# Three 64-partition loads issued by ScalarE, and the last quarter of the second weights issued by GpSimd inside tile 0's second product

## The chip, the core and the metric

The kernel runs on one core of a Trainium2 chip. The core's engines are TensorE (PE, matmuls; its weight loads are listed as PEld), VectorE (DVE), ScalarE (ACT), GpSimd (POOL) and SyncE (SP). They run their own instruction streams in order and wait for each other by semaphores. Transfers between HBM and the on-chip memory are started by an instruction on SP, ACT or POOL and are carried out by 16 DMA engines that all of them share. The profile names the queues by their issuer: q1 is SP's, q10 is ACT's (both "hardware_dynamic"), q0 is POOL's ("software_dynamic").

The metric is device time in microseconds (us), lower is better. Beside the plain runs there is one profiled execution, from which all rows below come.

## What is computed

Attention in a sliding window, then a feed-forward block with the tanh form of GELU:

```python
# q, k, v: 8 batches x 8 heads x 576 positions x 64, fp32
scores = q @ k^T / 8;  scores = -1e9 where |i - j| > 32
attn = softmax(scores);  a = attn @ v
x = a.transpose(0, 2, 1, 3).reshape(4608, 512)
h = x @ w_in                      # w_in 512 x 2048
out = gelu_tanh(h) @ w_out        # w_out 2048 x 512
```

## The kernel before

The 4608 tokens are worked on in nine tiles of 512. While the second product (`gelu @ w_out`) of tile t runs on TensorE, the attention of batch t+1 is woven into it at fixed places. All engines' orders are written out by hand: what the Python code emits first on an engine runs first on it.

Inputs arrive in fp32 and are cast to fp16 on chip. `w_in` and `w_out` are loaded in four quarters of 1 MB each (`load_w_in`, `load_w_out`, lines 232 to 238) into fp32 staging buffers `wst` (a ring of five, shared with the values `vr`) and cast by `cast_w` (line 240, profile line L242) on DVE, ACT or POOL. Below, wo0 to wo3 are the four quarters of `w_out`; each holds four blocks of 128 rows, so wo2 holds blocks 8 to 11 and wo3 blocks 12 to 15. A quarter can be loaded in two halves of 512 KB; wo2b is the second half of wo2 (line 856), wo3a and wo3b are the halves of wo3 (lines 858 and 860).

All loads of the opening are issued by SP, except two of the very first (one of q, one of k), which ACT issues. Loads to 64 partitions carry the last 64 positions of a batch, 128 KB each in rows of 256 bytes: `vs(4)` loads those of v (`vt`, line 156), `tails_0("q")` those of q of batch 0 (`tr`, line 166), `tails_0("k")` those of k. In SP's order the stretch that matters reads:

```python
850    wo.append(load_w_out(1, stage_w()))          # wo1, 1 MB
851    qk(4)
852    tails_0("q")                                 # 64 partitions
853    wo.append(load_w_out(2, stage_w(), 0, 2))    # wo2a
854    qk(6)
855    vs(0)
856    load_w_out(2, wo[2], 2, 4)                   # wo2b
857    vs(1)
858    wo.append(load_w_out(3, stage_w(), 0, 2))    # wo3a
859    vs(2, 3)
860    load_w_out(3, wo[3], 2, 4)                   # wo3b
861    vs(4)                                        # 64 partitions
862    tails()
```

Here `qk(4)` is one 256 KB load of q and one of k for two heads of batch 1, and `vs(0)` to `vs(3)` are the four 256 KB loads of batch 1's values. After line 862 SP goes on to batch 2 (`load_qk(2)`).

Loads by SP and ACT share eight completion semaphores in turn, in the order in which they are recorded: each load waits, before it is issued, for the landing of the load eight places before it. So wo2b waits for wo1, and wo1 is what SP waits for before it can issue wo2b.

Tile 0's second product is 64 steps (`ffn_out_0`, profile line L691), one matmul each. `ORDER_0` (line 70) gives the order: four steps for each block of `w_out`, so step i below 48 needs block i // 4, roughly; blocks 12 to 15 are needed from step 48 on (12 and 13 from 48, 14 and 15 from 56). `PLAN_0` (line 53) says before which step each other action comes. Those that matter here: `w1` at 15 (casts of wo1), `k2` at 19 (casts of q and k of batch 1, and POOL's cast of batch 0's q tail, L334), `w2` at 28 (blocks 8 and 9 of wo2), `t-1` at 29 and `s-1` at 34 (batch 0's tail), `n0` at 34 (sums of batch 1, their logarithm and reciprocal on ACT), `e0`, `e1`, `e2`, `e3` at 35, 43, 47, 52 (POOL's casts of the values, L329), `k3` at 37, `w5` at 38 (blocks 10 on POOL and 11 on ACT), `r3` at 41, `s3` and `w3` at 47 (blocks 12 on DVE and 13 on POOL), `d0` to `d3` (DVE copies of the values), `u3` at 55 (blocks 14 on POOL and 15 on ACT), `p0` at 57 (batch 1's weighted values), `e4` at 58 (POOL's cast of `vt`).

Of the kernel before, what the change touches and what calls it, by code (L numbers as in the profile page):

```python
# [78 lines left out]
def kernel(  # L79
# [9 lines left out]
    nc = tc.nc  # L89
    B, H, S, D = q.shape  # L90
# [12 lines left out]
    def load_table(which):  # L103
        nc.scalar.add_instruction(mybir.InstLoadActFuncSet(  # L104
            name=nc.get_next_instruction_name(), act_func_set_id=which, ins=[], outs=[]))
# [29 lines left out]
    raws, vrs = {}, {}  # L135

    def load_early(b):


        qr = rawp.tile([128, H, 256], FP32, name="qr")  # L140
        kr = rawp.tile([128, H, 256], FP32, name="kr")
        raws[b] = [qr, kr, None]

        def qk(h0, queues=(nc.sync, nc.sync)):
            for src, dst, queue in zip((q, k), (qr, kr), queues):
                queue.dma_start(
                    dst[:, h0:h0 + 2, :],
                    src[b, h0:h0 + 2, 0:512, :].rearrange("h (p j) d -> p h (j d)", j=4))

        def vs(*cs):  # L150
            if len(raws[b]) < 4:
                raws[b].append(stage.tile([128, 4, H, 64], FP32, name="vr", tag="stage"))
                raws[b].append(tailp.tile([64, H, 64], FP32, name="vt", tag="vt"))
            for c in cs:
                if c == 4:
                    nc.sync.dma_start(raws[b][4], v[b, :, 512:S, :].rearrange("h p d -> p h d"))
                else:
                    nc.sync.dma_start(raws[b][3][:, c, :, :],
                                      v[b, :, 128 * c:128 * c + 128, :].rearrange("h p d -> p h d"))

        def tails(which="qk"):
            if raws[b][2] is None:
                raws[b][2] = tailp.tile([128, H, 64], FP32, name="tr", tag="tr")
            tr = raws[b][2]
            if "q" in which:
                nc.sync.dma_start(tr[0:64, :, :], q[b, :, 512:576, :].rearrange("h s d -> s h d"))
            if "k" in which:
                nc.sync.dma_start(tr[64:128, :, :], k[b, :, 512:576, :].rearrange("h s d -> s h d"))

        return qk, tails, vs  # L170

    def load_qk(b):
# [54 lines left out]
    w_out_v = moe_w_out.rearrange("(c p) f -> p c f", p=128)  # L227

    def stage_w():
        return stage.tile([128, 4, 512], FP32, name="wst", tag="stage")  # L230
# [2 lines left out]
        nc.sync.dma_start(w[:, c0:c1, :], w_in_v[:, c0:c1, 512 * i:512 * i + 512])  # L233
        return w

    def load_w_out(i, w, c0=0, c1=4):
        nc.sync.dma_start(w[:, c0:c1, :], w_out_v[:, 4 * i + c0:4 * i + c1, :])
        return w

    def cast_w(w, dst, on_dve=(0, 1), cs=range(4), on_act=()):  # L240
        for c in cs:
            (nc.scalar.copy if c in on_act else nc.vector.tensor_copy if c in on_dve else nc.gpsimd.tensor_copy)(  # L242
                dst[:, c, :], w[:, c, :])

    qk, tails_0, vs = load_early(0)
# [3 lines left out]
    qk(4)  # L249
    qk(6)  # L250
    load_table(exp_set)
    def v_of_pair(g, hs=(0, 1)):
        for h in (2 * g + x for x in hs):
            nc.sync.dma_start(raws[0][3][:, :, h, :], v[0, h, 0:512, :].rearrange("(c p) d -> p c d", p=128))  # L254

    vs(4)
    for g in range(3):
        v_of_pair(g)
    wi = [stage_w()]
    load_w_in(0, wi[0], 0, 2)  # L260
    for x in range(2):
        v_of_pair(3, (x,))
        load_w_in(0, wi[0], 2 + x, 3 + x)
# [43 lines left out]
    def band_out():  # L307
        blocks(nc.vector.tensor_copy, band, full, even, (0, 1, 24, 8), (24, 3, 32, 0), (120, 1, 24, 0))
        blocks(nc.vector.tensor_copy, band, full, odd, (0, 1, 40, -8), (40, 2, 32, 0), (104, 1, 40, 0))
# [9 lines left out]
    def cast_early(b, pr, engs):  # L319
        for src, dst, eng in zip(raws[b][0:2], halfs[b][0:2], engs):  # L320
            if eng is not None:
                eng.tensor_copy(dst[:, pr, :, :, :].rearrange("p j h d -> p h j d"),
                                src[:, 2 * pr:2 * pr + 2, :].rearrange("p h (j d) -> p h j d", j=4))
# [78 lines left out]
    def open_and_turn(b):  # L402
        cast_open(b)
        turn_queries(b, raws[b][0], halfs[b][0], 0, 128)
# [74 lines left out]
    def weigh(b, g, pair=None):  # L479
        pe = groups.pop((b, g))  # L480
        if pair is not None:
            od = psS.tile([128, 2, 512], FP32, name="ps_od", tag=f"S{pair}")
            o, d = od[:, 0, :], od[:, 1, :]
        else:
            o = psO.tile([128, 512], FP32, name="ps_o", tag="O")
            d = psO.tile([128, 512], FP32, name="ps_d", tag="D")
        sum_up(b, g, d, pe)
        times(b, g, o, pe)
        return o, d
# [36 lines left out]
    def ffn_in(t, n, d0=0, d1=4, then=True):  # L526
        fc = column(t, n)
        if t not in gTs:
            gTs[t] = gp.tile([128, NF, 512], FP16, name="gT", tag="gT")
        if d0 == 0:  # L530
            if t == 0:
                i = n % 8
                if i in (4, 6):
                    phs["S"] = psS.tile([128, 2, 512], FP32, name="ph2", tag=f"S{i // 2 - 2}")
                phs[fc] = psO.tile([128, 512], FP32, name="ph", tag="DO"[i]) if i < 2 else \
                    bank(i - 2) if i < 4 else phs["S"][:, i % 2, :]
            else:
                i = 3 if n in (1, 2) else 0 if n == 0 else (2, 1, 0)[n % 3] if t < NT - 2 else (2, 0)[n % 2 if n > 3 else 0]
                if n == 1:
                    phs["S"] = psS.tile([128, 2, 512], FP32, name="ph3", tag="S0")  # L540
                phs[fc] = bank(i) if i < 2 else phs["S"][:, n - 1, :] if i == 3 else \
                    psO.tile([128, 512], FP32, name="ph", tag="D")
        ph = phs[fc]
        for dc in range(d0, d1):
            nc.tensor.matmul(ph, w_in16[:, dc, fc * 128:fc * 128 + 128],  # L545
                             xT[:, dc, t * 512 % RING:t * 512 % RING + 512],
                             start=(dc == 0), stop=(dc == 3))
        if d1 == 4 and then:
            gelu(t, n)

    def gelu(t, n):
        fc = column(t, n)
        nc.scalar.activation(gTs[t][:, fc, :], phs[fc], AF.Gelu_apprx_tanh)  # L553
        if t and n % 4 == 3:
            sums(t, n // 4)
# [263 lines left out]
    values(0, nc.gpsimd.tensor_copy)  # L819
    values(1, nc.gpsimd.tensor_copy)  # L820

    qk, tails, vs = load_early(1)
    qk(0)
    wo = [load_w_out(0, stage_w())]
    qk(2)

# [21 lines left out]
    cast_w(wi[1], w_in16[:, :, 512:1024], (0, 2))  # L848
    cast_w(wi[2], w_in16[:, :, 1024:1536], (0, 2))
    wo.append(load_w_out(1, stage_w()))  # L850
    qk(4)
    tails_0("q")
    wo.append(load_w_out(2, stage_w(), 0, 2))
    qk(6)
    vs(0)
    load_w_out(2, wo[2], 2, 4)
    vs(1)
    wo.append(load_w_out(3, stage_w(), 0, 2))
    vs(2, 3)
    load_w_out(3, wo[3], 2, 4)  # L860
    vs(4)
    tails()

    cast_open(1)
# [2 lines left out]
    def quarter(i, *dcs):  # L867
        for dc in dcs:
            for n in range(4 * i, 4 * i + 4):
                ffn_in(0, n, dc, dc + 1, then=False)  # L870
        if 3 in dcs:
            for n in range(4 * i, 4 * i + 4):
                gelu(0, n)

    quarter(1, 0, 1, 2, 3)
    cast_w(wi[3], w_in16[:, :, 1536:2048], (0, 2))
    quarter(2, 0, 1, 2, 3)
    cast_early(1, 0, split)
    band_out()
    quarter(3, 0, 1)  # L880
# [13 lines left out]
    for t in range(NT):  # L894
        b = t + 1
# [55 lines left out]
        for i in range(113 if t else 65):  # L951
# [3 lines left out]
            if t == 1 and i == 94:  # L955
                for c in range(4):
                    nc.gpsimd.tensor_copy(Vs[1][:, c, :, :], vrs[3][:, c, :, :])
            if t == 1 and i == 98:
                open_and_turn(3)
            for act in plan.get(i, "").split():  # L960
                kind, at = act[0], int(act[act.index("@") + 1:]) if "@" in act else None
                g = int(act[1:].split("@")[0])
                if kind == "w":
                    if g == 3:
                        cast_w(wo[g], w_out16[:, 12:16, :], cs=(0, 1), on_dve=(0,))
                    else:
                        cast_w(wo[g % 3], w_out16[:, 4 * (g % 3):4 * (g % 3) + 4, :], on_act=(1, 3),
                               cs={1: range(4), 2: (0, 1), 5: (2, 3)}[g])
# [41 lines left out]
                elif kind == "v":  # L1010
                    bb, gg = group(g)
                    o, d = weigh(bb, gg, at)
# [61 lines left out]
```

## Time and profile before

| what | value |
|---|---|
| runs | 299.73, 299.79, 300.87 us; median 299.79 us |
| profiled execution, device time | 298.71 us |
| its span, first to last instruction | 297.0 us |
| its granted TensorE clock | 0.999 |
| PE busy | 287.1 us (97%) |
| DVE, ACT, POOL busy | 209.2 us (70%), 196.4 us (66%), 89.4 us (30%) |
| share of the 16 DMA engines' span: q1, q0, q10 | 61.6%, 23.0%, 1.1% |
| moved | 51.01 MB, 172 GB/s on average |

Stretches of the opening, from the view by windows (busy us of each engine in the stretch, then the DMA engines' busy share and rate):

| stretch, us | PE | DVE | ACT | POOL | DMA share | GB/s |
|---|---|---|---|---|---|---|
| 0 to 4 | 2.74 | 1.55 | 2.10 | 1.78 | 0.44 | 144 |
| 8 to 12 | 3.65 | 2.87 | 3.45 | 1.82 | 1.28 | 248 |
| 20 to 24 | 4.00 | 1.54 | 2.61 | 1.65 | 1.06 | 400 |
| 32 to 34 | 1.41 | 0.86 | 1.29 | 0.49 | 1.07 | 372 |
| 38 to 40 | 1.96 | 1.64 | 1.46 | 0.46 | 1.09 | 245 |
| 42 to 44 | 2.00 | 1.31 | 1.41 | 0.00 | 1.13 | 307 |
| 46 to 48 | 1.52 | 0.22 | 1.66 | 1.22 | 1.18 | 276 |
| 48 to 50 | 2.00 | 1.82 | 0.57 | 0.97 | 0.67 | 153 |
| 52 to 54 | 1.49 | 1.81 | 2.00 | 0.75 | 1.11 | 219 |

The page reads so: engine busy times are sums over instructions; the DMA share is the time that packets took as a share of the 16 engines' time, and can exceed 1 because packets overlap. In the timeline a row is: start, duration, engine, line, operation, output and input, count, and in brackets the idle time of that engine before the row and what ended it. SPq, ACTq and POOLq rows are the issues of loads and stores, not the transfers. Some SPq durations hold waiting as well as issuing.

### The profile page before, as it was taken

The page shows a single profiled execution, that of the slowest core. Times are in us where ns is not written, and L with a number is a line of the kernel's source. Part 1 is how long each engine was busy: PE and PEld are TensorE (multiplying, and loading weights), DVE is VectorE, ACT ScalarE, POOL GpSimd, SP SyncE. Part 2 cuts the span into 40 slices and gives each one's busy share as a digit, 9 for nine tenths or more (in the row PEclk, how much of TensorE's full clock was granted, in tenths as well). Part 3 has the DMA queues.
Part 4 walks back from the last instruction along what each step waited for, and adds up shares of the span by engine and source line. Part 5 has one row for each costly group of instructions (what it writes and reads, how often), then busy time and mean ns, then how long its engine had stood idle before and what let it go on. Part 6 is the DMA issues. An engine that isn't in the chain of part 4 may idle for free.

```text
span 297.0 us, 7282 instructions
## 1 busy us (share of the span) xinstructions
PE 287.1 (97%) x2949; PEld 184.7 (62%) x2949; DVE 209.2 (70%) x466; ACT 196.4 (66%) x315; POOL 89.4 (30%) x141
## 2 busy tenths in 40 slices
PE   7889999999999999999999999999999999999993
PEld 3534444446874587458844884488547867786783
DVE  4662475997986676868686879576966776964772
ACT  4876756778587876678657965695669557705800
POOL 3435415201407731406080606060800050015000
PEclk9999999999999999999999999999999999999999
DMA  7999999989999998989997997999594040004013
GB/s 216 263 297 383 366 280 263 264 178 202 291 192 191 235 233 156 145 167 244 150 193 116 253 145 158 142 227 170 102 175 38 0 116 29 2 13 131 0 35 109
DMA packets 116615, 51.01 MB, mean 172 GB/s; under 512 B 98391, under 2 KB 110167, under 8 KB 116582
## 3 DMA queue, kind: packets, MB, share of 16 engines
q1 hardware_dynamic: 91684, 38.67, 61.6%
q0 software_dynamic: 23776, 10.83, 23.0%
q10 hardware_dynamic: 1122, 1.06, 1.1%
q8 instruction: 23, 0.38, 0.6%
q14 instruction: 10, 0.08, 0.1%
HBM read 36.70 MB, written 9.44 MB: 155 GB/s over the span
## 4 chain that ended last, share of the span: by engine, by line
PE 80%; DMA 13%; DVE 2%; SPq 2%; ACT 1%; issue 1%; POOL 0%
PE mm L719 32%; PE mm L545 17%; PE ph L545 15%; DMA wst<-in_moe_w_out_dram 7%; DMA wst<-in_moe_w_in_dram 5%; PE pu L597 3%; PE ps_s L436 3%; PE ps_d L463 2%; DMA tr<-in_k_dram 2%; PE ps_o L473 2%; SPq L254 2%; PE mm L597 1%; PE ps_od L473 1%; PE ps_od L463 1%; PE mm L691 1%; PE py L719 1%
## 5 line engine op out<-in xcount | busy, mean ns | idle before, releaser
L545 PEld LDWEIGHTS <-w_in 128*128 128x128 f16 x512 | 49.7, 98 | 56.9 <-POOL w_in L835 0.5
L545 PE MATMUL ph<-xT,w_in 128*128 128x512 f16 x256 | 64.1, 379 | 0.4 <-POOL w_in L835 0.4
L545 PE MATMUL mm<-xT,w_in 128*128 128x512 f16 x256 | 64.1, 379 | 0.0
L681 POOL DMA_DIRECT2D out_dram<-y x55 | 32.3, 597 | 83.8 <-DVE y L748 75.5
L553 ACT ACTIVATE gT<-mm 128x512 f16<-128x512 f32 x60 | 35.6, 598 | 33.1 <-PE mm L545 32.5
L719 PEld LDWEIGHTS <-s 128*128 128x128 f16 x512 | 49.3, 98 | 7.1 <-DVE s L662 0.6
L719 PE MATMUL mm<-t,s 128*128 128x256 f16 x376 | 45.2, 273 | 0.3 <-DVE y L732 0.2
L662 DVE TENSOR_TENSOR s<-gT 128x512 f16<-128x512 f16 x64 | 27.2, 426 | 19.0 <-ACT gT L553 18.8
L719 PEld LDWEIGHTS <-gT 128*128 128x128 f16 x384 | 36.2, 98 | 6.5
L553 ACT ACTIVATE gT<-ph 128x512 f16<-128x512 f32 x58 | 32.2, 600 | 10.9 <-PE ph L545 10.9
L449 ACT ACTIVATE pe<-ps_s 128x960 f16<-128x960 f32 (+1 forms) x31 | 29.5, 974 | 13.9 <-PE ps_s L436 13.8
L719 PE MATMUL mm<-w_out,gT 128*128 128x256 f16 x256 | 32.6, 273 | 0.0
L104 ACT ACT_TABLE_LOAD x18 | 23.1, 1283 | 2.2 <-issue 1.9
L498 ACT ACTIVATE lt<-ps_d 128x480 f32<-128x480 f32 (+2 forms) x28 | 15.6, 556 | 10.4 <-PE ps_d L463 6.9
L499 ACT ACTIVATE lt<-lt 128x480 f32<-128x480 f32 (+3 forms) x36 | 21.1, 585 | 1.1
L458 DVE TENSOR_TENSOR pe<-pe,band 128x960 f16<-128x960 f16 x28 | 18.6, 683 | 2.3 <-ACT pe L449 2.3
L473 PEld LDWEIGHTS <-V 128*64 128x64 f16 x520 | 13.8, 111 | 6.3 <-DVE V L218 1.2
L719 PE MATMUL mm<-t,gT 128*128 128x256 f16 x128 | 16.1, 273 | 0.0
L208 POOL DMA_DIRECT2D V<-in_v_dram x16 | 14.3, 909 | 1.1 <-POOL after L953 0.4
L662 DVE TENSOR_TENSOR s<-s,gT 128x512 f16<-128x512 f16 x32 | 13.9, 434 | 1.1
L719 PE MATMUL mm<-w_out,s 128*128 128x256 f16 x120 | 14.6, 273 | 0.0
L508 DVE TENSOR_TENSOR xT<-ps_o,lt 128x480 f16<-128x480 f32 (+5 forms) x26 | 13.4, 536 | 1.1 <-PE ps_o L473 1.1
(146 smaller groups left out, 387.1 us busy)
## 6 DMA issues: line engine op xcount, KB each, us to landing
kr<-in_k_dram SPq DMA_DIRECT2D x31, 256.0 KB, 10.0
qr<-in_q_dram SPq DMA_DIRECT2D x6, 1024.0 KB, 6.9
wst<-in_moe_w_in_dram SPq DMA_DIRECT2D x7, 512.0 KB, 8.4
wst<-in_moe_w_out_dram SPq DMA_DIRECT2D x2, 1024.0 KB, 11.6
wst<-in_moe_w_out_dram SPq DMA_DIRECT2D x4, 512.0 KB, 5.8
qr<-in_v_dram SPq DMA_DIRECT2D x8, 256.0 KB, 5.6
V<-in_v_dram POOLq DMA_DIRECT2D x16, 128.0 KB, 8.8
qr<-in_q_dram SPq DMA_DIRECT2D x7, 256.0 KB, 6.9
```

The costliest lines, as they stand in the source:

```text
L104: nc.scalar.add_instruction(mybir.InstLoadActFuncSet(name=nc.get_next_instruction_name(), act_func_set_id=which, ins=[], outs=[]))
L208: nc.gpsimd.dma_start(V[:, c, :, :], v[b, :, 128 * c:128 * c + 128, :].rearrange("h p d -> p h d"))
L449: nc.scalar.activation(pe, ps[:, :, 0:w], AF.Exp, scale=SCALE)
L458: nc.vector.tensor_tensor(pe, pe, m.rearrange("k (o j) p -> k o j p", o=1).broadcast_to(list(pe.shape)), op=ALU.mult)
L473: nc.tensor.matmul(o[64 * h:64 * h + 64, cols].rearrange("d (j p) -> d j p", j=4)[:, :, p0 - q0:p1 - q0], Vs[b % 2][:, slot, 2 * pr + h, : ...
L498: nc.scalar.activation(lt[:, 0:n], d[:, 0:n], AF.Ln)
L499: nc.scalar.activation(lt[:, 0:n], lt[:, 0:n], AF.Exp, scale=-1.0)
L545: nc.tensor.matmul(ph, w_in16[:, dc, fc * 128:fc * 128 + 128], xT[:, dc, t * 512 % RING:t * 512 % RING + 512], start=(dc == 0), stop=(dc = ...
L553: nc.scalar.activation(gTs[t][:, fc, :], phs[fc], AF.Gelu_apprx_tanh)
L662: nc.vector.tensor_tensor(dst, x, y, op=op)
L681: eng.dma_start(out_v[b, j, q0 + p:q0 + p + e, cols], yo[m:m + e, cols])
L719: nc.tensor.matmul(pys["apart"][:, 0:256] if apart else py[:, blk, :], lhsT, wino[w][:, f, :], start=(new and i % (8 if one else 16) == 0) ...
```

## The change

Three loads to 64 partitions go from SP to ACT. The one of batch 0's v tail is recorded after the first table load instead of just before it in SP's order; that of batch 0's q tail stands in ACT's order after the twelve GELUs of the first three quarters of tile 0's first product; that of batch 1's v tail stands before step 30 of tile 0's second product. The two halves of wo3 go from SP to POOL, before step 20 of the same product, so after POOL's cast of the q tail (`k2`, step 19). Every other load keeps its place in SP's order. `vs` and `tails` and `load_w_out` get the issuing queue as an argument.

```diff
-        def vs(*cs):
+        def vs(*cs, queue=nc.sync):
...
                 if c == 4:
-                    nc.sync.dma_start(raws[b][4], v[b, :, 512:S, :].rearrange("h p d -> p h d"))
+                    queue.dma_start(raws[b][4], v[b, :, 512:S, :].rearrange("h p d -> p h d"))
...
-        def tails(which="qk"):
+        def tails(which="qk", queue=nc.sync):
...
             if "q" in which:
-                nc.sync.dma_start(tr[0:64, :, :], q[b, :, 512:576, :].rearrange("h s d -> s h d"))
+                queue.dma_start(tr[0:64, :, :], q[b, :, 512:576, :].rearrange("h s d -> s h d"))
...
-    def load_w_out(i, w, c0=0, c1=4):
-        nc.sync.dma_start(w[:, c0:c1, :], w_out_v[:, 4 * i + c0:4 * i + c1, :])
+    def load_w_out(i, w, c0=0, c1=4, queue=nc.sync):
+        queue.dma_start(w[:, c0:c1, :], w_out_v[:, 4 * i + c0:4 * i + c1, :])
...
     load_table(exp_set)
+    vs(4, queue=nc.scalar)
...
-    vs(4)
     for g in range(3):
         v_of_pair(g)
...
-    qk, tails, vs = load_early(1)
+    qk, tails, vs_1 = load_early(1)
...
     qk(4)
-    tails_0("q")
     wo.append(load_w_out(2, stage_w(), 0, 2))
     qk(6)
-    vs(0)
+    vs_1(0)
     load_w_out(2, wo[2], 2, 4)
-    vs(1)
-    wo.append(load_w_out(3, stage_w(), 0, 2))
-    vs(2, 3)
-    load_w_out(3, wo[3], 2, 4)
-    vs(4)
+    vs_1(1)
+    wo.append(stage_w())
+    vs_1(2, 3)
     tails()
...
     quarter(2, 0, 1, 2, 3)
+    tails_0("q", nc.scalar)
     cast_early(1, 0, split)
...
+            if t == 0 and i == 20:
+                load_w_out(3, wo[3], 0, 2, nc.gpsimd)
+                load_w_out(3, wo[3], 2, 4, nc.gpsimd)
+            if t == 0 and i == 30:
+                vs_1(4, queue=nc.scalar)
```

## The prediction

> **What bounds the kernel now.** I read the chain that ended last first. By engine (page, part 4):
>
> ```profile
> PE 80%; DMA 13%; DVE 2%; SPq 2%; ACT 1%; issue 1%; POOL 0%
> ```
>
> TensorE carries it but for 13% of transfers. In order of time, these lie in the opening alone:
>
> ```profile
> 17.35 9.12 DMA wst<-in_moe_w_in_dram
> 26.55 11.24 DMA wst<-in_moe_w_out_dram
> 37.81 8.40 DMA wst<-in_moe_w_out_dram
> 46.26 0.62 POOL w_out L242
> 46.92 0.38 PE mm L691
> ```
>
> (Start, length, what.) wo1 lands at 37.8, which lets SP issue wo2b; wo2b lands 8.4 us later, POOL casts block 10 in 0.62 us, and step 40 starts at 46.92. From there the chain is TensorE's. The timeline of TensorE shows what its waits in tile 0's second product are worth:
>
> ```profile
> 33.96 0.60 PE L691 MATMUL mm<-w_out,gT 128*128 128x512 f16 x2 [0.59 <-DVE w_out L242]
> ...
> 46.92 0.38 PE L691 MATMUL mm<-w_out,gT 128*128 128x512 f16 x1 [0.48 <-POOL w_out L242]
> ...
> 52.85 0.38 PE L691 MATMUL mm<-w_out,gT 128*128 128x512 f16 x1 [0.40 <-POOL w_out L242]
> ```
>
> The three (wo0, block 10 of wo2, block 14 of wo3) sum to 1.47 us: all that better loading here can give back. SP's own timeline:
>
> ```profile
> 37.81 2.18 SPq L237 DMA_DIRECT2D wst<-in_moe_w_out_dram  x1
> 40.04 1.06 SPq L158 DMA_DIRECT2D vr<-in_v_dram  x1
> 41.20 2.28 SPq L237 DMA_DIRECT2D wst<-in_moe_w_out_dram  x1
> 43.53 2.64 SPq L158 DMA_DIRECT2D vr<-in_v_dram  x2
> 46.21 2.42 SPq L237 DMA_DIRECT2D wst<-in_moe_w_out_dram  x1
> ```
>
> The reader is to see the order: wo2b (37.81) stands in front of both halves of wo3 (41.20, 46.21), and q1 serves them in that order. Last, what q1 moved from 42 to 46.2, while wo2b was on its way (packets, MB, share of 16 engines):
>
> ```profile
> q1 hardware_dynamic: 1944, 1.26, 105.3%
> ```
>
> The DMA engines are full, at 0.30 MB a us. So transfers and their order bound step 40, not issuing.
>
> **Part by part: wo3 from POOL.** POOL's timeline says when it can issue:
>
> ```profile
> 37.85 0.61 POOL L242 CAST w_out<-wst 128x512 f16<-128x512 f32 x1 [1.97 <-DMA wst<-in_moe_w_out_dram]
> 40.94 0.60 POOL L334 CAST t<-tr 64x512 f16<-64x512 f32 x1 [2.47 <-DMA tr<-in_q_dram]
> ```
>
> The cast at 37.85 waits for wo1. L334 follows it, and waits no more: its tail now travels from about 31, and ACT's first loads were cast 3.8 to 4.6 us after issue (0.81 to 4.58, 1.35 to 5.92). So L334 ends at 39.1. Then the two issues: nearest rows 0.65 us (128 rows of 2 KB, L681) and 0.91 us (1024 rows of 256 B, L208); these have 256 rows of 2 KB, I take 0.65, so 1.3 (at most 1.8) us. POOL idles 3.04 us ahead of its next cast (44.58), which hides them; without that idle they would delay `e0`, not TensorE. The buffer of wo3 came free at 30.2 (last casts of `w_in`), so the issues wait for nothing.
>
> From issue to transfer, POOL's stores show 1 to 3 us (117.40, with 0.38 MB moved from 118 to 120; 76.42, with only 0.08 MB before 80). The transfer thus starts between 40.3 and 42; I take 42. wo2b then still has 1.26 MB of q1 ahead of and in itself. How do q0 and q1 share? The nearest row is POOL's store beside SP's k loads. From 78 to 80, nearly alone:
>
> ```profile
> q1 hardware_dynamic: 1688, 0.50, 109.5%
> ```
>
> and from 80 to 82, together:
>
> ```profile
> q1 hardware_dynamic: 951, 0.24, 54.3%
> q0 software_dynamic: 133, 0.43, 53.4%
> ```
>
> q0 took half of the engines' time and q1's bytes halved. At these rates wo3 (1.05 MB at 0.215 MB a us) needs 4.9 us, to 46.9. In that time q1 moves half of 0.30 x 4.9, some 0.74 MB; the other 0.52 MB takes 1.7 us more. wo2b lands at 48.6 instead of 46.2: +2.4 us. Upper bound: all of wo3 first, 1.05 MB at the 0.37 MB a us of 32 to 34, +2.8. Lower bound: q0 starts after 46.2, 0; below nothing, -0.5, if the tail's 128 KB, which stood before wo2b, moved in otherwise unused engine time. I take 2.4, as the start can slip to 44 and still leave +2.2. TensorE already waits at step 40, so all of this counts: it starts at 46.92 + 2.4 = 49.3.
>
> The Trainium skill's page "DMA: Bandwidth & Descriptors", section "Issuing engines are not separate DMA queues", says that loads of all issuers run on the same 16 engines and interleave, and that more issuers save issue time only; that speaks against this change, and the windows above agree (q1 from 0.50 to 0.24 MB). By that rule with equal turns the sum would be near the upper bound, by the rows it is the 2.4.
>
> What it saves: wo3 lands at 46.9, before steps 48 and 56 want it, so the 0.40 at 52.85 goes.
>
> **What comes behind.** With wo3 gone, batch 1's values follow wo2b in q1: 256 KB each, 0.85 us apiece at 0.30 MB a us, 49.5, 50.3 and 51.2. POOL's last value cast (0.61 to 1.09 us) is then over by 52.3 and DVE's last two copies (0.29 to 0.60 each) by 53.5; `p0`, at 53.16 before, comes at 55.2. This has 1.7 us of cover. q of batch 2 is issued earlier than 50.70; its cast at 58.75 waited for no transfer.
>
> **SP's freed places.** The five issues took 0.61 (4.95), 1.57 (30.12), 2.28, 2.42 and 0.61 (48.67) us. Those after wo2b free nothing that TensorE waits for; the first two lie before it, but wo2b's issue waits for wo1's landing (SP idles 0.77 us before 37.81), and bytes before wo1 stay the same, less nothing and plus the q tail, which now runs beside wo1 instead of behind it: 128 KB, 0.35 us at 0.37 MB a us. That delays block 4 (cast 37.94 to 38.74, step 16 at 38.86) by up to 0.35 us, and is swallowed by the wait at step 40, as is any delay ahead of it.
>
> **The three issues on ACT.** Each 0.50 us (ACTq rows at 0.81 and 1.35: 0.50, 0.49). The v tail of batch 0 goes at 3.16, before six copies; ACT idles 1.11 us before its next row (5.89). It now runs beside the last q and k loads instead of behind them: 512 packets at 760 a us (q1, 10 to 12 us: 1520 packets in 2 us), 0.67 us against the same gain for the values behind; bounds -0.6 to +0.7, and I take 0. The q tail goes at 30.8 into idle times of 0.87 and 0.71 us (before 31.68 and 32.98); its semaphore is that of q's first load of batch 1, cast at 30.15. So 0, and still 0 at SP's 1.57 us for the same load. The v tail of batch 1 adds a wait: it shares its semaphore with `qk(6)`'s k load, eight places earlier. Before, that landed by 44.5 (its cast at 44.51 idled for nothing); at half rate from 42 I put it at 45.5. ACT stands still from 44.1 to 46.0. Queued behind: exp of the tail (0.60), two Ln (1.03), two Exp (1.09), block 11's cast (0.62), so until 49.4; step 44 stood 1.31 us behind step 40 (48.23 and 46.92), so it wants block 11 at 49.3 + 1.3 = 50.6. Hidden, with 1.2 us to spare.
>
> **Sum.** +2.4 - 0.40 + 0 = +2.0 us. The profiled execution (span 297.0, 1.7 around it, 298.71) becomes 300.7. The median of the runs lies 1.08 above it; I carry the difference over: 299.79 + 2.0 = 301.8 us. About 0.5%, 1.5 us, is what a measurement of this kernel can tell from no change, so the bounds are 298.3 and 301.3.
>
> **Rivals.** (1) *wo2b is not disturbed, not slower.* If POOL's transfers start later than 46, or q0 gets scraps, wo2b keeps its landing and only 0.40 (or, with the tail's bytes gone from its front, 0.88) is saved: 298.9 to 299.4; with a part of the delay left, up to 300. It decides from a start of 45.5 on, since what wo2b has left then is under 0.7 us. For it: value loads issued by POOL at 133.99 show no q0 packet before 138. Against: those have four times the rows, and the stores started sooner.
> (2) *ACT becomes the wait.* If k of `qk(6)` lands after 46.7, the 1.2 us are used up and step 44 or `s3` waits for ACT on top: +0.5 to +1.5, 302.3 to 303.3. For it: ACT has four results queued there that TensorE or DVE want. Against: the load stands ahead of wo2b by 0.75 MB.
> (3) *SP's issuing paced the stream.* Then all loads come earlier, the waits of 0.59, 0.48, 0.40 and one of 0.44 at 18.06 go: 299.79 - 1.9 = 297.9. For it: the DMA engines dip (77% from 18 to 20, 67% from 48 to 50). Against: 95% and more in every us from 26 to 48.
>
> **How the numbers follow.** Forecast 0.61 (300.9 to 302.6; some 0.14 of it under 301.3), rival 1 0.19, rival 2 0.14, rival 3 0.06. Slower by over 0.5%: 0.47 + 0.14 = 0.61; within: 0.14 + 0.19 = 0.33; faster: 0.06. Range 299.2 to 303.3: it leaves out rival 3, half of rival 1 and the end of rival 2. The forecast's own range is that of its bounds, 300.9 to 302.6.
>
> **What would show it.** TensorE's wait before step 40 near 2.9 us with POOL's cast of block 10 behind wo2b; q0 with about half of the engines from 42 to 47; no wait at block 14; POOL issuing L237 near 39 to 40.5; ACT idle from 44 to 46 before the exp of the tail. I am wrong if wo2b lands before 47, if q0 starts after 45, or if TensorE's longest wait stands elsewhere.

## The result: 0.58% slower, and the profile after

| what | before | after |
|---|---|---|
| median of the runs, us | 299.35 (298.74 to 300.87) | 300.87 (299.91 to 303.29) |
| ratio, 95% interval | | 1.0058 [1.0039, 1.0077] |
| profiled execution, us | 298.71 | 300.14 |
| its span, us | 297.0 | 298.4 |
| step 0 of tile 0's second product, us | 33.96 | 34.59 |
| first matmul of tile 1, us | 56.06 | 57.28 |
| second product of the last tile begins, us | 279.41 | 280.62 |

The change costs about 1.7 us (0.58% of 299.35; the two medians lie 1.5 us apart). In the profiled executions 1.22 us of the difference is there when tile 1 begins, and it is the same at the last tile (1.21). So the place is the opening, up to 57 us. The chain that ended last, by engine, has slightly less transfer in it than before (11% for 13%) and more VectorE (3% for 2%):

```profile
PE 81%; DMA 11%; DVE 3%; SPq 1%; ACT 1%; issue 1%
```

TensorE's timeline after, in the stretch shown of before:

```profile
34.59 0.60 PE L691 MATMUL mm<-w_out,gT 128*128 128x512 f16 x2 [0.60 <-DVE w_out L242]
...
41.33 0.40 PE L350 MATMUL pt<-idn,q 128*128 128x128 f16 x4 [0.28 <-DVE q L322]
...
54.09 0.38 PE L691 MATMUL mm<-w_out,gT 128*128 128x512 f16 x1 [1.06 <-POOL w_out L242]
54.39 1.44 PE L473 MATMUL ps_od<-pe,V 128*64 128x96 f16 x56
```

The wait of 0.48 us before step 40 has gone; the prediction had made it 2.9. The wait before step 56 (block 14) has grown from 0.40 to 1.06. POOL's timeline after says how that came about:

```profile
40.94 1.64 POOL L237 DMA_DIRECT2D wst<-in_moe_w_out_dram  x2
...
45.79 0.76 POOL L242 CAST w_out<-wst 128x512 f16<-128x512 f32 x1 [1.04 <-DMA wst<-in_moe_w_out_dram]
48.44 0.61 POOL L329 CAST V<-vr 128x512 f16<-128x512 f32 x1 [1.89 <-DMA vr<-in_v_dram]
48.99 0.61 POOL L242 CAST w_out<-wst 128x512 f16<-128x512 f32 x1
51.48 0.70 POOL L329 CAST V<-vr 128x512 f16<-128x512 f32 x1 [1.87 <-DMA vr<-in_v_dram]
52.72 0.70 POOL L329 CAST V<-vr 128x512 f16<-128x512 f32 x1 [0.54 <-DMA vr<-in_v_dram]
53.37 0.67 POOL L242 CAST w_out<-wst 128x512 f16<-128x512 f32 x1
53.98 0.67 POOL L334 CAST t<-tr 128x512 f16<-128x512 f32 x1
54.60 0.66 POOL L326 CAST V<-vt 64x512 f16<-64x512 f32 x1
```

Block 10 is cast at 45.79, not later than before (46.26): wo2b was not made late. The values v2 and v3 (51.48 and 52.72) come late; before, both were cast in one stretch from 49.66 to 51.56. SP began to issue v2 and v3 earlier than before (at 41.11 and 43.32, before at 43.53 and 44.22), so issuing doesn't explain it. Block 14 (53.37) waits for no transfer any more, it stands in POOL's order behind v3. So the 1 MB that moved to q0 came in time, and what it overtook did not.

Which of these late things set the time? The chain of waits of after, from the last scores of batch 1 on (start, length, what):

```profile
49.66 0.36 PE ps_s L436 x16
50.05 0.98 ACT pe L449
51.05 0.66 DVE pe L458
...
51.74 0.59 DVE V L222
...
54.19 0.61 DVE V L224
...
54.85 0.98 PE ps_od L473 x42
```

It doesn't run through block 14 at all. After VectorE's mask of the last pair (L458) come six copies of the values (L222, L224), one behind the other, and 42 of the 56 matmuls of `p0` and `p2` wait for the last one. The wait of 1.06 us on TensorE lies beside this chain. VectorE's timeline of before has the same six copies:

```profile
50.43 0.66 DVE L458 TENSOR_TENSOR pe<-pe,band 128x960 f16<-128x960 f16 x1 [0.55 <-ACT pe L449]
51.12 0.59 DVE L222 COPY V<-V 64x512 f16<-64x512 f16 x1
51.72 0.28 DVE L224 COPY V<-V 64x512 f16<-64x512 f16 x1
52.03 0.29 DVE L222 COPY V<-V 64x512 f16<-64x512 f16 x1
52.34 0.60 DVE L224 COPY V<-V 64x512 f16<-64x512 f16 x1
52.97 0.29 DVE L222 COPY V<-V 64x512 f16<-64x512 f16 x1
53.28 0.29 DVE L224 COPY V<-V 64x512 f16<-64x512 f16 x1
```

and that of after, at the same distance from the mask:

```profile
51.74 0.59 DVE L222 COPY V<-V 64x512 f16<-64x512 f16 x1
52.34 0.28 DVE L224 COPY V<-V 64x512 f16<-64x512 f16 x1
52.65 0.29 DVE L222 COPY V<-V 64x512 f16<-64x512 f16 x1
52.96 0.60 DVE L224 COPY V<-V 64x512 f16<-64x512 f16 x1
53.59 0.59 DVE L222 COPY V<-V 64x512 f16<-64x512 f16 x1
54.19 0.60 DVE L224 COPY V<-V 64x512 f16<-64x512 f16 x1
```

Two equal copies take 0.29 us or 0.59 us. The long ones are those that begin while a POOL cast is already running: in after the casts end at 52.18, 53.42, 54.04 and 54.65 and the long copies at 52.33, 53.56, 54.18 and 54.79, each 0.14 or 0.15 us behind. In before there are two long ones and in after four, since POOL's late casts (v3, block 14, the q and k tails) now lie beside the last copies: 2.95 us of copies instead of 2.34. The page "SBUF — State Buffer" of the Trainium skill, section "SBUF: two separate sides", says that GpSimd and a VectorE instruction in a two-port mode share a pair of ports, which the one that starts first holds for its whole instruction while the other is blocked; these rows agree, as the copies end at a fixed distance behind the casts.

The account of the two profiled executions up to tile 1 is then: 0.62 us up to the mask (51.05 less 50.43), 0.61 us in the copies, 1.22 at tile 1. The first 0.62 is the later start of step 0 (0.63). That part can't be put down to the change by the profiles alone: step 0 began between 33.28 and 34.96 in the kernels below, and two of the latest (34.96 and 34.51) belong to kernels that touch nothing which runs before step 0.

Between step 0 and the mask the two kernels take the same time (16.47 and 16.46 us), although the wait of 0.48 before step 40 has gone. The move of batch 0's q tail explains it, as e2_qtail below shows. wo1 lands 4.50 us after step 0 instead of 3.83, and the tail's cast on POOL (L334), which waits no more, now runs beside VectorE's cast of q (0.83 us instead of 0.41). The transposes of that q begin 6.74 us after step 0 instead of 6.20. TensorE comes later to step 40 and finds block 10 there: one wait was exchanged for another.

### The profile page after: what moved, and what is told of

Read it like the earlier page. It is cut to its first block, busy times and chain, and to the rows that moved or that the text cites. A ratio compares the mean times of both kernels' runs of the same rounds, so it can differ in the third digit from the quotient of the medians.

```text
span 298.4 us, 7279 instructions
## 1 busy us (share of the span) xinstructions
PE 287.5 (96%) x2949; PEld 184.1 (62%) x2949; DVE 210.2 (70%) x466; ACT 196.4 (66%) x315; POOL 90.7 (30%) x143
## 4 chain that ended last, share of the span: by engine, by line
PE 81%; DMA 11%; DVE 3%; SPq 1%; ACT 1%; issue 1%
PE mm L719 32%; PE mm L545 17%; PE ph L545 15%; DMA wst<-in_moe_w_in_dram 5%; DMA wst<-in_moe_w_out_dram 4%; PE ps_s L436 3%; PE pu L597 3%; PE ps_d L463 2%; DMA kr<-in_k_dram 2%; PE ps_o L473 2%; PE py L691 1%; PE mm L691 1%; PE mm L597 1%; SPq L255 1%; PE ps_od L463 1%; PE ps_od L473 1%
## 5 line engine op out<-in xcount | busy, mean ns | idle before, releaser
L458 DVE TENSOR_TENSOR pe<-pe,band 128x960 f16<-128x960 f16 x28 | 18.9, 694 | 2.6 <-ACT pe L449 2.6
L473 PEld LDWEIGHTS <-V 128*64 128x64 f16 x520 | 13.8, 112 | 6.6 <-issue 2.1
```

The lines of the kernel that those rows point to most:

```text
L458: nc.vector.tensor_tensor(pe, pe, m.rearrange("k (o j) p -> k o j p", o=1).broadcast_to(list(pe.shape)), op=ALU.mult)
L473: nc.tensor.matmul(o[64 * h:64 * h + 64, cols].rearrange("d (j p) -> d j p", j=4)[:, :, p0 - q0:p1 - q0], Vs[b % 2][:, slot, 2 * pr + h, : ...
```

## The experiments

A table of all of them first. "Copies end" and "tile 1" are counted from step 0 of the same profiled execution, in us. The last column says, from the chain of waits in the stretch ahead of tile 1, what it came through last: the copies behind the mask, a transfer, or ACT. Each ratio is to runs of before on the same chip.

| kernel | ratio to before, 95% interval | copies, sum | copies end | tile 1 | chain comes through |
|---|---|---|---|---|---|
| before | | 2.34 | 19.61 | 22.10 | mask, copies |
| after | 1.0058 [1.0039, 1.0077] | 2.95 | 20.20 | 22.69 | mask, copies |
| e1_open | 0.9996 [0.9978, 1.0014] | 2.16 | 20.25 | 22.83 | mask, copies |
| e2_qtail | 0.9994 [0.9971, 1.0017] | 2.03 | 19.53 | 22.27 | ACT's logarithms, block 15 |
| e3_vtail | 1.0032 [1.0008, 1.0056] | 2.36 | 19.47 | 21.97 | wo3b, block 14 |
| e4_wo3 | 1.0027 [1.0004, 1.0051] | 2.65 | 20.51 | 23.00 | v3, block 14 |
| e5_three | 1.0029 [1.0005, 1.0052] | 2.32 | 20.03 | 22.82 | wo3b, block 14 |
| f1_cast14 | 1.0019 [0.9999, 1.0040] | 2.03 | 20.76 | 23.25 | v3, copies |
| f2_early | 1.0085 [1.0052, 1.0118] | 3.03 | 22.17 | 24.67 | mask, copies |
| f3_vt_back | 1.0010 [0.9983, 1.0037] | 2.63 | 20.04 | 22.53 | v3, block 14 |
| g1_order | 1.0036 [1.0009, 1.0062] | 2.62 | 20.71 | 23.21 | mask, copies |
| g2_two | 0.9989 [0.9969, 1.0009] | 2.03 | 19.41 | 21.93 | TensorE's sums (L463), copies |
| g3_vt_late | 1.0059 [1.0037, 1.0082] | 2.94 | 20.29 | 22.78 | copies (TensorE's last wait); the chain runs on to the v tail in tile 1 |
| g4_mix | 1.0004 [0.9979, 1.0029] | 2.11 | 19.97 | 22.46 | v3, block 14 |

Tile 1 begins 2.49 to 2.58 us after the last copy in all rows but e2_qtail (2.74) and e5_three (2.79), also where the chain comes through block 14. So the copies and block 14 end nearly together: two paths, of which either can be the last. They are tied: in e3_vtail, e4_wo3, f3_vt_back and g4_mix the copy before the last begins while block 14's cast runs and ends 0.14 or 0.15 us behind it, so a late block 14 makes the copies late too. One profiled execution of each kernel scatters by some tenths here, and e1_open's ratio shows that its 22.83 is no loss; the chain's way says more than the column of times.

### The four parts, one at a time

**e1_open**: batch 0's v tail alone goes to ACT.

```diff
     load_table(exp_set)
+    vs(4, queue=nc.scalar)
...
-    vs(4)
```

> Only batch 0's v tail is issued by ACT; all else as before. Theory O (the 0.63 us that the changed kernel is late at step 0 of tile 0's second product comes from the opening, where this load took turns of the first q and k loads): ratio 1.001 to 1.003, third-last cast of w_in near 27.1 instead of 26.5, step 0 near 34.6. Theory N (that lateness is scatter between executions and belongs to no part): ratio 0.999 to 1.001, step 0 anywhere between 33.9 and 34.7. The prediction took 0.

Measured 0.9996 [0.9978, 1.0014]: nothing. Step 0 began at 33.95, as before.

**e2_qtail**: batch 0's q tail alone goes to ACT.

```diff
-    tails_0("q")
...
     quarter(2, 0, 1, 2, 3)
+    tails_0("q", nc.scalar)
```

> Only batch 0's q tail is issued by ACT. By the prediction: 0 (its 128 KB runs beside wo1 instead of behind it, wo1 lands up to 0.35 us later, 37.8 to 38.2). Rival: the tail's 512 packets of 256 B no longer stand in q1 ahead of wo2a, wo2b, so block 10's cast comes 0.4 to 0.9 us earlier (45.4 to 45.9), the 0.48 us wait at step 40 goes and the ratio is 0.998 to 0.9985.

Measured 0.9994 [0.9971, 1.0017]: nothing either. Block 10 was cast at 46.31 (before 46.26). The wait before step 40 went all the same, since TensorE came later: wo1 landed 4.56 us after step 0 (before 3.83), and the transposes of q (L350) began 6.79 us after it. In all nine kernels with this edit that distance is 6.74 to 6.89 us, in the five without it 6.19 or 6.20. So the move costs TensorE more than half a microsecond there, and the wait before step 40 takes it up.

**e3_vtail**: batch 1's v tail alone goes to ACT, before step 30.

```diff
-    vs(4)
+    vs_1 = vs
...
+            if t == 0 and i == 30:
+                vs_1(4, queue=nc.scalar)
```

> Only batch 1's v tail is issued by ACT, before step 30. By the prediction: 0 with ACT standing still up to 1.9 us for its semaphore. Rival V: its 512 packets, from about 46 on, run beside the last values v2 and v3 in q1 instead of behind them, POOL's casts of v2 and v3 come 0.3 to 0.7 us later, and block 14's cast behind them too: wait at step 56 of 0.7 to 1.0 instead of 0.40, ratio 1.001 to 1.002.

Measured 1.0032 [1.0008, 1.0056]. ACT didn't stand still: the load was issued at 43.06 in 0.73 us. TensorE's wait before step 56 was 0.92 instead of 0.40, as wo3b landed later: block 14 was cast at 52.93 after 0.98 us of waiting for its transfer, before at 52.05 after 0.49. From 46 to 50 us q10 carried 0.13 MB and q1 0.70 MB, where q1 alone had carried 0.85: the tail's bytes now travel ahead of wo3b instead of behind it. The chain of waits of this kernel comes through it (start, length, what):

```profile
46.24 6.64 DMA wst<-in_moe_w_out_dram
52.93 0.62 POOL w_out L242
...
53.60 0.38 PE mm L691
53.98 1.05 PE ps_od L473 x56
```

Yet step 0 to tile 1 took 21.97 us, no more than before (there was no wait before step 40 here), and this profiled execution (301.56 us) lost its time elsewhere:

```profile
226.77 0.62 PE L436 MATMUL ps_s<-QT,KT 64*64 64x96 f16 x32 [2.09 <-DMA KT<-k]
```

That is a wait for a transpose of k, 170 us behind the edit. Such waits (0.6 to 2.1 us) were found in e4_wo3 and f1_cast14 too, at 134 us, so they don't belong to this part alone.

**e4_wo3**: wo3 alone goes to POOL.

```diff
-    wo.append(load_w_out(3, stage_w(), 0, 2))
+    wo.append(stage_w())
...
-    load_w_out(3, wo[3], 2, 4)
...
+            if t == 0 and i == 20:
+                load_w_out(3, wo[3], 0, 2, nc.gpsimd)
+                load_w_out(3, wo[3], 2, 4, nc.gpsimd)
```

> Only the two halves of wo3 are issued by POOL, before step 20. Theory A, the prediction's: q0 takes half of the engines while wo2b is on its way, step 40 is 2 us or more late, ratio 1.005 to 1.009. Theory B, from the trace of the changed kernel: wo2b is untouched (block 10's cast before 46.5), but q0's megabyte goes ahead of v1, v2 and v3; POOL casts in order, so block 14, landed by 50, waits behind the casts of v2 and v3 until after 53; the only long wait is at step 56, 0.9 to 1.5 us, ratio 1.001 to 1.004.

Measured 1.0027 [1.0004, 1.0051]. v2 and v3 were cast at 51.68 and 52.49, block 14 behind them at 53.20, and the copies took 2.65 us. Waits of 0.93 before step 40 and 1.03 before step 56. Block 10 was cast at 46.69, 0.43 later than before and past the 46.5 of theory B; but in e1_open, which leaves wo3 alone, it was cast at 46.73, so this can't be put down to POOL's queue.

**e5_three**: the three loads go to ACT, wo3 stays on SP.

```diff
     load_table(exp_set)
+    vs(4, queue=nc.scalar)
...
-    vs(4)
...
-    tails_0("q")
...
-    vs(4)
+    vs_1 = vs
...
+    tails_0("q", nc.scalar)
...
+            if t == 0 and i == 30:
+                vs_1(4, queue=nc.scalar)
```

> The three 64-partition loads by ACT, wo3 left on SP. If the parts add: ratio 1.002 to 1.004, wait before step 56 of 0.7 to 1.0. If the q tail's move gives the v tail's cost back: 0.999 to 1.001.

Measured 1.0029 [1.0005, 1.0052], which is e3_vtail's ratio: the two other loads add nothing. Block 14 was cast at 52.98 after 1.19 us of waiting for wo3b, though step 0 had begun 0.20 us earlier than before, and again the chain comes through wo3b. In before and in g2_two, where SP issues the tail behind wo3b, it comes through the copies.

### What carries the cost of wo3

**f1_cast14**: as after, with block 14 cast by ACT before step 53, so that it no longer stands behind v3 on POOL.

```diff
+            if t == 0 and i == 53:
+                nc.scalar.copy(w_out16[:, 14, :], wo[3][:, 2, :])
...
-                    cast_w(wo[g], w_out16[:, 12:16, :], on_act=(3,), cs=(2, 3))
+                    cast_w(wo[g], w_out16[:, 12:16, :], on_act=(3,), cs=(3,))
```

> The changed kernel, with one edit: block 14 is cast by ACT before step 53 instead of by POOL behind the casts of v2 and v3. Theory B (wo3 has landed by 50 and only POOL's order makes step 56 wait): the 1.06 us wait before step 56 shrinks to under 0.3, a wait at p0 for the values may take 0.2 to 0.5 of it, ratio to before 1.001 to 1.004. Theory A' (wo3 itself lands late): the wait stays at 0.8 or more, with ACT idle ahead of the cast until the load lands, ratio 1.005 or more.

Measured 1.0019 [0.9999, 1.0040]. The wait before step 56 went, and TensorE waited for the copies instead:

```profile
54.72 0.98 PE L473 MATMUL ps_od<-pe,V 128*64 128x64 f16 x46 [1.22 <-DVE V L224]
```

So block 14's place on POOL chose which instruction shows the wait; in the profile nothing was won (23.25 us for 22.69). The ratio is lower than after's, with intervals that just touch, so a small gain isn't excluded. In this execution v2 and v3 were cast at 51.95 and 53.12, so two copies waited for data (0.87 and 0.57 us); only the last one, 0.60 us long, began beside a POOL cast.

**f2_early**: as after, with wo3 issued before step 2 instead of step 20.

```diff
-            if t == 0 and i == 20:
+            if t == 0 and i == 2:
```

> The changed kernel with POOL issuing wo3 before its cast of wo1 (before step 2 of the product) instead of after its cast of the q tail, so near 36 us instead of 41. Theory A, the sharing as the prediction priced it (q0 halves q1 while it is at work; it only started too late here to touch wo2b): q0 moves from about 38.5 on, wo2b lands after 48, block 10's cast comes 1.5 to 2.8 us later than in the changed kernel's 45.8, the long wait stands before step 40, ratio 1.008 to 1.014. Theory A0 (q0 does not hold q1's older loads up): block 10's cast stays before 46.5 and the ratio at 1.004 to 1.007.

Measured 1.0085 [1.0052, 1.0118]. Now the mechanism that was predicted is there. POOL's and TensorE's timelines of this kernel:

```profile
35.20 1.64 POOL L237 DMA_DIRECT2D wst<-in_moe_w_out_dram  x2
...
47.45 0.61 POOL L242 CAST w_out<-wst 128x512 f16<-128x512 f32 x1 [0.85 <-DMA wst<-in_moe_w_out_dram]
```

```profile
48.12 0.38 PE L691 MATMUL mm<-w_out,gT 128*128 128x512 f16 x1 [1.71 <-POOL w_out L242]
```

wo2b's block 10 is late and step 40 waits 1.71 us. From 40 to 42 us the queues stood so (packets, MB, share of 16 engines):

```profile
q0 software_dynamic: 172, 0.64, 87.7%
q1 hardware_dynamic: 171, 0.11, 18.4%
```

One packet of q0 for one of q1, and with packets of some 3.7 KB against 0.6 KB q0 gets 6 of 7 bytes. The page "DMA: Bandwidth & Descriptors" of the Trainium skill, section "Queues, rings and completion order", says that each DMA engine takes turns between its queues by packets; this window agrees. Other windows don't show equal counts: in f2_early from 42 to 44 us there were 96 packets of q0 and 635 of q1, and in after, from 44 to 46 us, 156 and 386, so there q1 got more turns, but in the latter again few bytes:

```profile
q0 software_dynamic: 156, 0.59, 78.6%
q1 hardware_dynamic: 386, 0.14, 27.0%
```

**g1_order**: before, with SP issuing both halves of wo3 ahead of v1, v2 and v3. Nothing on POOL or ACT.

```diff
-    vs(1)
     wo.append(load_w_out(3, stage_w(), 0, 2))
-    vs(2, 3)
     load_w_out(3, wo[3], 2, 4)
+    vs(1)
+    vs(2, 3)
```

> The kernel before, with one edit: SP issues both halves of wo3 ahead of batch 1's values v1, v2, v3 instead of between and behind them. No POOL issue, no ACT issue. Theory R (what POOL's queue did to the changed kernel is reorder: 1 MB of 2 KB rows served ahead of the 256 B rows of the values, which then run alone and slowly): v2 and v3 cast near 51 to 52.7 as in the changed kernel instead of 49.7 and 50.6, wait at step 56 or at p0 of 0.7 to 1.3, ratio 1.001 to 1.004. Theory Q (the software queue itself is the cost): v2 and v3 within 0.5 us of before, ratio 0.998 to 1.001.

Measured 1.0036 [1.0009, 1.0062]. POOL's timeline of this kernel:

```profile
47.62 0.61 POOL L242 CAST w_out<-wst 128x512 f16<-128x512 f32 x1 [0.54 <-DMA wst<-in_moe_w_out_dram]
51.22 0.62 POOL L329 CAST V<-vr 128x512 f16<-128x512 f32 x1 [2.99 <-DMA vr<-in_v_dram]
51.77 0.62 POOL L242 CAST w_out<-wst 128x512 f16<-128x512 f32 x1
52.33 1.67 POOL L329 CAST V<-vr 128x512 f16<-128x512 f32 x2
```

With wo3 in front on the same queue, all three values are late, and tile 1 begins 23.21 us after step 0. The chain shows three pieces: block 10 cast 0.36 us later from step 0 than in before (e1_open shows as much without this edit), the mask 1.11 instead of 0.66 us beside POOL's casts, and 0.28 us more of copies. So the loss needs no second queue: it is enough that wo3 overtakes the values. The order of before, with v1 ahead of wo3a and v2, v3 between the halves, was worth that much.

**g4_mix**: the two free edits of e1_open and e2_qtail, and wo3b between v2 and v3.

```diff
-    vs(2, 3)
+    vs(2)
     load_w_out(3, wo[3], 2, 4)
+    vs(3)
```

> As the kernel with two loads by ACT, and SP issues wo3b between v2 and v3 instead of behind v3, so that rows of 2 KB run beside rows of 256 B. A try at a faster version: theory R gives 0.996 to 0.999 if the last needed load lands earlier than 52.0; 0.999 to 1.002 if TensorE is by then bound by its own work or v3 becomes the late one.

Measured 1.0004 [0.9979, 1.0029]. v3 came at 52.23 and the copies' end at 19.97 after step 0, for 19.41 in g2_two below: one overtaken value shows in the profile (the chain comes through v3), but not in the ratio.

### What carries the cost of batch 1's v tail

**f3_vt_back**: as after, with that tail back on SP.

```diff
-    vs_1(2, 3)
+    vs(2, 3)
+    vs(4)
...
-            if t == 0 and i == 30:
-                vs_1(4, queue=nc.scalar)
```

> The changed kernel with batch 1's v tail back on SP. If the parts add (1.0032 for this tail alone, 1.0027 for wo3 alone, nothing for the other two): ratio 1.002 to 1.004, and v2 and v3 cast 0.3 to 0.7 us earlier than the 51.5 and 52.7 of the changed kernel. If the tail alone cost its 0.32% by scatter only: ratio 1.005 to 1.007.

Measured 1.0010 [0.9983, 1.0037], for after's 1.0058. v2 and v3 were cast at 50.34 and 51.70, 16.89 and 18.25 us after step 0, for 16.89 and 18.13 in after; the gain of 0.3 to 0.7 us that was expected for them did not come. The last copy took 0.29 us instead of 0.60: with the v tail again in front of them in SP's order, the q and k tails came later, and POOL's cast of them (L334) began after the copies (20.11 after step 0, copies' end 20.04) instead of beside the last one. That is 0.31 us in the copies, of which 0.16 is left at tile 1 (22.53 for 22.69).

**g2_two**: before, with only the two edits of e1_open and e2_qtail.

```diff
     load_table(exp_set)
+    vs(4, queue=nc.scalar)
...
-    vs(4)
...
-    tails_0("q")
...
+    tails_0("q", nc.scalar)
```

> The kernel before with only the first two of the three loads by ACT (batch 0's v tail and q tail). Theory of parts: each alone was 0.9996 and 0.9994, so 0.998 to 1.001; block 10 cast near 46, waits at steps 40 and 56 under 0.3 each. If 1.002 or more, the parts do not add and the third load was not the costly one.

Measured 0.9989 [0.9969, 1.0009]: no loss, and no proven gain. No version here beats before.

**g3_vt_late**: as after, with the v tail issued before step 57 instead of step 30, so that it is out of the way of v2 and v3.

```diff
-            if t == 0 and i == 30:
+            if t == 0 and i == 57:
                 vs_1(4, queue=nc.scalar)
```

> The changed kernel with ACT's issue of batch 1's v tail moved from before step 30 to before step 57 of the product, when all other loads of the stage have landed. Theory T (its place in time cost 0.3 to 0.5%, as its rows took turns from the values): ratio 1.000 to 1.003, v3 cast before 52.2. If the queue or the wait on ACT cost it: 1.004 to 1.007 as the changed kernel.

Measured 1.0059 [1.0037, 1.0082]. The idea that the tail costs only by its place in time fell: this place is no better. v2 did come sooner (cast at 50.58, 16.77 after step 0 for 16.89), but the q and k tails stayed early, their cast ran beside the copies (2.94 us), and the late tail brought something new. POOL's timeline:

```profile
60.50 0.67 POOL L326 CAST V<-vt 64x512 f16<-64x512 f32 x1 [7.17 <-DMA vt<-in_v_dram]
```

This cast now falls beside VectorE's weight combinations (the one from 60.62 took 1.63 us, the next one 1.21), and tile 1's first product took 14.75 us instead of 14.34 in before. A late tail and an early tail have the same ratio, with different rows.

## Why the prediction was right in size and wrong in its steps

It said 301.8 us, +2.0 us or 0.67%. The runs gave +0.58%, 1.7 us. The direction came true and the size nearly: the median of 300.87 lies just under the forecast's own range (300.9 to 302.6) and within the stated one. The step that was to carry it did not come, so the nearness of the number is luck.

**When q0 starts** (taken: 42). POOL issued from 40.94 to 42.58, later than the 39 to 40.5 of the text, as wo1 landed 1.3 us later in this execution. q0's first packets are found in the window from 43 to 44 (0.12 MB). The estimate of 1 to 3 us from issue to transfer holds here (2.1), but not everywhere: in f3_vt_back it was 3.5 us and in f2_early 4.5.

**wo2b has 1.26 MB before it: the step that failed.** From 42 us to block 10's cast at 45.79, q1 moved some 0.6 MB in after, and wo2b was there. The 1.26 MB was what q1 moved in that time in before, and it was read as work that all stood ahead of wo2b. The packets of that stretch in before show that it didn't:

```profile
DMA packets 1946, 1.29 MB, mean 306 GB/s; under 512 B 1495, under 2 KB 1523, under 8 KB 1944
```

Rows of values have 256 bytes, rows of q and k 1 KB, rows of weights 2 KB. The 1495 shortest packets are at most 0.38 MB and the next 28 some 0.03, so q1's 1.26 MB held about 0.85 MB of weights. The first half of wo2 was there by 42.11, when VectorE cast block 8 without waiting, and wo2b has only 0.52 MB. The other 0.33 MB, or more, must be wo3a, issued at 41.20, behind wo2b: transfers of one queue overlap. So the sentence that q1 "serves them in that order" was the false premise, and the clause that a start at 44 would still cost 2.2 us fell with it: with a start near 43 wo2b's block 10 was cast 6.68 us after SP began to issue the load, for 8.45 in before.

**How the queues share** (taken: halves). Over 42 to 47 us q0 did take 49.8% and q1 53.0% of the engines' time, but not evenly: nothing before 43, then 78.6% for 27.0% from 44 to 46. With an earlier start q0 does delay wo2b, as f2_early shows, where step 40 waits 1.71 us; the forecast was near 2.9.

**0.40 saved at step 56.** By the chain of before it was not simply there to be had. In before the chain of waits reaches the last 40 of the 56 matmuls of L473 at 53.62, from VectorE's last copy, which ended at 53.57; the wait of 0.40 at 52.85 lay beside it. An earlier block 14 could at most have freed the copy at 52.34 from its cast (0.60 instead of 0.29 us), and only if no other cast of POOL had moved there; no run tests that alone. f1_cast14 removes the wait of after at that place and shows one of 1.22 us for the copies.

**The values behind: "1.7 us of cover".** This was a real step of the sum, put at 0, and it is the term that was mis-sized. The three landings were given as 49.5, 50.3 and 51.2, at 0.30 MB a us; the casts came at 48.44, 51.48 and 52.72. Once wo3 is out of q1, only 256-byte rows are left there, and these moved at 0.12 to 0.15 MB a us from 47 to 50 us, beside 0.02 to 0.07 of q10's rows of the same length. The prediction had a row for this and did not use it here: the 760 packets a us from 10 to 12 us, by which a value load of 1024 rows takes 1.35 us instead of the 0.85 that it put down. From 50 to 52 us the engines weren't even full; the transfer view of after gives, in 40 slices (tenths) and for q1:

```profile
DMA  9989777676656565644553333211111114567799
...
q1 hardware_dynamic: 768, 0.19, 53.1%
```

The reader is to see a transfer trailing out: the share falls from 9 to 1 tenth while v3 isn't there yet. From 42 to 52 us, after moved 2.48 MB (q1 1.30, q0 1.05, q10 0.13) and before 2.67, at the same engine time (99.6% and 99.5%). And the cover itself was counted from a `p0` that step 40 had pushed to 55.2. Without that push there was none: the copies already set it.

**The three loads on ACT** (put at 0). For two of them that was right in sum: the q tail delayed wo1 by more than the 0.35 us put down (0.7 in e2_qtail, counted from step 0), and the wait before step 40 swallowed it, as the text said. For batch 1's v tail the prediction priced the wait on ACT; that wait did not come (the exp of the tail began at 45.72, when TensorE had its input). It priced neither the tail's own bytes ahead of what SP has queued, nor what SP then issues earlier. Three pairs of ratios speak for a cost: e3_vtail against before +0.32%, e5_three against g2_two +0.40%, after against f3_vt_back +0.48%, each with some 0.3% of doubt. wo3 on POOL gives +0.27% (e4_wo3), +0.21% (f3_vt_back against g2_two) and +0.29% (after against e5_three), with the same doubt; of these three only the first is clear of noise by itself. The sums agree with 0.58%. For wo3 the rows above show how: values that come late, and casts that collide with the copies. For the tail the profiles show two ways: with wo3 on SP, its bytes make wo3b late, and the chain comes through it (e3_vtail, e5_three); with wo3 on POOL, 0.31 us by one more collision, 0.16 of it left at tile 1 (f3_vt_back). The rest of its 1.0 to 1.4 us is in the runs alone. The middle half of e3_vtail's runs spans 299.97 to 301.72 us, that of before on the same chip 299.24 to 300.12, so the edit moves the runs and widens them. Whether waits like the one at 226.77 become more frequent by it stays open.

**The rivals.** Rival 1 described what happened to wo2b; its condition (a start from 45.5 on) was too strict, and its time (298.9 to 300) left out the values. Rival 2 (ACT becomes the wait) and rival 3 (all loads come earlier) did not happen: there is no wait for ACT in the second product, and step 0 came no earlier. Of the signs that were to show the forecast, q0 with about half of the engines from 42 to 47 was there (49.8%); the wait near 2.9 us before step 40, no wait at block 14, and ACT idle from 44 to 46 were absent, and POOL issued after 40.5. Two of the three signs of being wrong came: wo2b landed before 47, and TensorE's longest wait stood at step 56. The number came out near because one cost was exchanged for another of similar size.

## What to carry to other kernels

Before a wait is counted as a gain, look for the chain that runs beside it and ends in the same place: here 0.40 us of waiting for weights lay beside six copies, for the last of which 40 matmuls of the same stretch waited anyway. When a load leaves a queue, price what stays behind by its own rows: what moves at 0.30 MB a us with long rows among them moved at 0.17 to 0.19 when nearly all rows were of 256 bytes (after, 48 to 50 us, q1 and q10 together; before, 10 to 12 us). And where one engine's late work shares a resource with the engine on the path, moving the load that releases it moves the collision, not only the wait.

## What the runs showed of the hardware that had not been expected

- A copy of 64 x 512 in fp16 on VectorE took 0.28 or 0.29 us alone. When it began while a GpSimd cast was running it took 0.41 to 0.60 us and ended 0.14 to 0.16 us after that cast, in each of the seven cases of before and after (the seventh, of 0.41 us, began at 49.35 in after, late within its cast). One that began 0.02 us ahead of a cast (52.03 in before) kept its 0.29.
- GpSimd's loads of wo3 moved their first packet 2.1 to 4.5 us after their issue, with the engines full: 2.1 in after (issued from 40.94), 2.6 in e4_wo3 (41.51), 3.5 in f3_vt_back (39.95), 4.5 in f2_early (35.20). What sets this time stays open.
- How two queues shared the engines changed from window to window: q0, with packets of some 3.7 KB, took 87.7% to q1's 18.4% (f2_early, 40 to 42 us) and 78.6% to 27.0% (after, 44 to 46 us), but 46.9% to 54.8% in f2_early from 42 to 44 us.
- Transfers of one queue overlapped: by the packets' lengths about 0.33 MB of wo3a moved while wo2b, issued 3.4 us ahead of it, had not landed.
